# Sliding-window attention with a SwiGLU block: K and Q loaded six tokens per partition and put in order by the evictions, blocks of 512 and 256 tokens, one 3-bank PSUM ring

## The chip, the cores and the metric

The kernel runs on one core of one Trainium2 chip. The metric is the device time of one execution in microseconds; lower is better. The span of a profiled execution is some 2 us shorter than its device time. Stage times below are read from profiles, comparisons of kernels from device times.

## The reference

```python
# q, k, v: (4 batches, 8 heads, 768 tokens, 64), float32, drawn as randn * 0.1; n_sink = 4, window = 128
def _attn_ref(q, k, v, n_sink, window):
    scores = scale * np.matmul(q, k.transpose(0, 1, 3, 2))
    keep = is_sink | in_window            # the first 4 keys, and the last 128
    a = softmax(where(keep, scores, -1e9))
    return np.matmul(a, v)

def _moe_ref(x, w_gate, w_val, w_out):    # 3072 tokens, 512 -> 1536 -> 512
    g = x @ w_gate
    return (silu(g) * (x @ w_val)) @ w_out
```

## The kernel before

The work goes in groups of 256 tokens of one batch (12 groups). A group's K and Q are loaded as bf16 with 128 tokens on the partitions, transposed by TensorE for two heads at a time (step T), evicted to `kqT`, and used for scores (S), sink scores (K), probabilities times V (PV) and the transpose of the result (X) that the feed-forward reads. After a prologue with groups 0 and 1, the feed-forward of 512 tokens runs with the attention of the next two groups woven into its steps. In the traces each engine executes its instructions in program order: in the kernel before, VectorE's later work stands behind one multiply that waits 40.6 us.

```python
    ps_f = pool("ps_f", 3, True)       # gate, value and down outputs
    ps_s = pool("ps_s", 1, True)       # scores, two banks
    ps_o = pool("ps_o", 2, True)       # PV outputs
    ps_t = pool("ps_t", 1, True)       # T, K and X: one bank
    # ... (the queue of GpSimd, in order:)
    load_group(0, split=2)             # K, Q, V of 256 tokens: runs of 64 values
    load_group(1)
    load_gate(0); load_gate(1); load_gate(2); load_gate(3)     # masks are built in between
    load_group(2)
    for i in range(4):
        load_out(i)
    load_group(3)
    for b in range(B):                 # the sink values, last of all: 32 loads of 4 rows
        for h in range(H):
            nc.gpsimd.dma_start(vcs[b][h * NS:(h + 1) * NS, 0:D], v[b, h, 0:NS])
    # ...
    def step_T(g, p, on_dve=False):
        pt = ps_t.tile([P, 2, 2, P], BF16, tag="pt", name="pt")
        for i in range(2):
            for t in range(2):
                nc.tensor.transpose(
                    pt[:, i, t], nat[g][:, i, t, p * P:(p + 1) * P], ident)
        dst = kqT[b][:, p, :, c * 256:(c + 1) * 256].rearrange(
            "q i (t r) -> q i t r", t=2)
        if on_dve:
            nc.vector.tensor_copy(out=dst, in_=pt)
        else:
            nc.scalar.copy(out=dst, in_=pt)          # 128 partitions, dense
    # ...
    def step_ks(g):                    # after the first group of a batch
        # ...
        nc.vector.tensor_tensor(       # vsb: the sink values, one block per head
            vsbs[b],
            vcs[b].rearrange("q (o d) -> q o d", o=1).broadcast_to([P, H, D + 1]),
            diag_h.rearrange("q (h o) -> q h o", o=1).broadcast_to([P, H, D + 1]),
            op=ALU.mult)
```

The softmax here doesn't subtract the row's maximum and nothing guards it: scores larger than these inputs give would overflow.

## Time and profile before

| | before |
|---|---|
| device time, median | 327.62 us (3 runs, 327.23 to 330.12) |
| span of the profile | 325.2 us |
| first feed-forward matmul | 74.4 us |

In a line of the page's slices each digit is a fortieth of the span, in tenths of busy time. A group of instructions reads: line, engine, operation, output <- input, partitions x elements, count, then busy us and mean ns of one, then the idle time before them with its releasers. The prediction shows the slices, the waits and the stages. Two more lines of before, its evictions of the transposes, from the groups by shape:

```profile
L213 ACT COPY kqT<-pt 128x512 bf16<-128x512 bf16 x44 | 25.8, 585 | 54.6 <-PE pt L206 54.6
L211 DVE COPY kqT<-pt 128x512 bf16<-128x512 bf16 x4 | 1.7, 424 | 12.6 <-PE pt L206 12.6
```

### The profile page before, as it was taken

The numbers are of one execution on the slowest core, as the hardware profiler recorded it, in microseconds if no ns is written. First come the engines' busy times: TensorE is split into PE (matmuls) and PEld (weight loads), VectorE is DVE, ScalarE is ACT, GpSimd is POOL, SyncE is SP. The second block draws the span as 40 slices with busy tenths as digits, with TensorE's granted clock in tenths as the row PEclk, the third lists the DMA queues.
The fourth block names the chain that finished last, engine by engine and source line by source line (L and its number), as shares of the span: only waits on it lengthen the run. The fifth ranks groups of instructions, "written<-read, shape, count | busy, mean of one in ns | idle before, by whom it ended". The sixth has DMA issues, their size and how long they took to land.

```text
span 325.2 us, 4622 instructions
## 1 busy us (share of the span) xinstructions
PE 251.2 (77%) x1824; PEld 128.8 (40%) x1824; DVE 167.9 (52%) x352; ACT 127.2 (39%) x197; POOL 95.8 (29%) x142
## 2 busy tenths in 40 slices
PE   0420000576999988999979999799997999999995
PEld 0210000353454544555434545345453454544442
DVE  2200000663788526886158882378842688617830
ACT  1230000324665136762257541475514666223321
POOL 8996756996532006050042600000000000000000
PEclk9999999999999999999999999999999999999999
DMA  8999999099929129390149932100011000020002
GB/s 56 113 132 203 173 203 90 1 72 124 100 15 84 40 92 73 24 99 30 69 54 78 75 24 90 39 2 3 1 65 67 0 2 0 34 94 3 2 32 97
DMA packets 85268, 20.75 MB, mean 64 GB/s; under 512 B 76544, under 2 KB 82176, under 8 KB 85248
## 3 DMA queue, kind: packets, MB, share of 16 engines
q0 software_dynamic: 81792, 14.18, 55.3%
q1 hardware_dynamic: 3456, 6.29, 5.0%
q8 instruction: 14, 0.23, 0.3%
q14 instruction: 6, 0.05, 0.0%
HBM read 28.34 MB, written 6.29 MB: 107 GB/s over the span
## 4 chain that ended last, share of the span: by engine, by line
PE 63%; DVE 13%; DMA 9%; POOL 7%; ACT 5%; issue 2%; DVEq 0%; POOLq 0%
PE pd L363 18%; PE pv L348 16%; PE pg L340 15%; DVE ht L353 4%; PE o L286 4%; PE s L242 3%; PE pt L206 3%; DMA wg<-in_moe_w_gate_dram 3%; DMA va<-in_v_dram 3%; POOL kq L89 3%; DMA wo<-in_moe_w_out_dram 3%; DVE e L251 2%; DVE u L352 2%; ACT th L343 2%; PE px L304 2%
## 5 line engine op out<-in xcount | busy, mean ns | idle before, releaser
L340 PE MATMUL pg<-xT,wg 128*128 128x512 bf16 x288 | 73.9, 379 | 0.5 <-DVE xT L307 0.5
L348 PE MATMUL pv<-xT,wv 128*128 128x512 bf16 x288 | 74.1, 380 | 0.0
L352 DVE SCALAR_TENSOR_TENSOR u<-th,pg 128x512 bf16<-128x512 f32 x72 | 49.4, 686 | 40.8 <-ACT th L343 39.9
L343 ACT ACTIVATE th<-pg 128x512 f32<-128x512 f32 x72 | 43.0, 597 | 69.4 <-PE pg L340 69.4
L206 PE MATMUL pt<-ident,kq 128*128 128x128 bf16 x192 | 20.2, 233 | 61.2 <-DVE kqT L211 39.9
L363 PE MATMUL pd<-wo,ht 128*128 128x512 bf16 x288 | 65.6, 379 | 0.0
L353 DVE TENSOR_TENSOR ht<-u,pv 128x512 bf16<-128x512 bf16 x72 | 49.5, 688 | 24.1 <-PE pv L348 19.5
L247 ACT ACTIVATE e<-s 128x1024 bf16<-128x1024 f32 (+1 forms) x48 | 45.6, 950 | 9.9 <-PE s L242 9.3
L213 ACT COPY kqT<-pt 128x512 bf16<-128x512 bf16 x44 | 25.8, 585 | 54.6 <-PE pt L206 54.6
L89 POOL DMA_DIRECT2D kq<-in_k_dram x26 | 22.6, 882 | 77.7 <-PE pt L206 76.7
L340 PEld LDWEIGHTS <-wg 128*128 128x128 bf16 x288 | 28.2, 98 | 34.4 <-issue 0.6
L206 PEld LDWEIGHTS <-kq 128*128 128x128 bf16 x192 | 13.6, 103 | 67.6 <-issue 61.2
L363 PEld LDWEIGHTS <-ht 128*128 128x128 bf16 x288 | 27.4, 98 | 30.4
L367 ACT ACTIVATE ot<-pd 128x512 f32<-128x512 f32 x24 | 14.3, 597 | 60.3 <-PE pd L363 60.3
L348 PEld LDWEIGHTS <-wv 128*128 128x128 bf16 x288 | 25.0, 98 | 23.6 <-issue 3.6
L251 DVE TENSOR_TENSOR e<-e,mask 128x1024 bf16<-128x1024 bf16 (+1 forms) x48 | 30.6, 640 | 1.8 <-ACT e L247 1.8
L223 DVE TENSOR_TENSOR vsb<-vc,diag_h 128x520 bf16<-128x520 bf16 x4 | 2.8, 701 | 40.7 <-DMA vc<-in_v_dram 40.6
L89 POOL DMA_DIRECT2D kq<-in_q_dram x26 | 22.6, 885 | 0.8 <-DMA wv<-in_moe_w_val_dram 0.8
L242 PE MATMUL s<-kqT 64*128 64x128 bf16 (+1 forms) x256 | 19.6, 255 | 3.9 <-ACT e L247 3.9
L96 POOL DMA_DIRECT2D va<-in_v_dram x24 | 21.4, 915 | 3.7 <-DMA wo<-in_moe_w_out_dram 1.7
L292 DVE TENSOR_TENSOR xn<-o,rcp 128x256 bf16<-128x256 f32 x48 | 20.4, 425 | 1.7
L286 PEld LDWEIGHTS <-e 128*128 128x128 bf16 x352 | 17.7, 103 | 6.6 <-issue 0.9
(36 smaller groups left out, 126.0 us busy)
## 6 DMA issues: line engine op xcount, KB each, us to landing
out_dram<-ot SPq DMA_DIRECT2D x24, 256.0 KB, 2.0
va<-in_v_dram POOLq DMA_DIRECT2D x24, 128.0 KB, 4.5
kq<-in_k_dram POOLq DMA_DIRECT2D x22, 128.0 KB, 4.2
kq<-in_q_dram POOLq DMA_DIRECT2D x22, 128.0 KB, 4.7
wg<-in_moe_w_gate_dram POOLq DMA_DIRECT2D x4, 384.0 KB, 7.7
wv<-in_moe_w_val_dram POOLq DMA_DIRECT2D x4, 384.0 KB, 8.9
wo<-in_moe_w_out_dram POOLq DMA_DIRECT2D x4, 384.0 KB, 9.1
vc<-in_v_dram POOLq DMA_DIRECT2D x32, 0.5 KB, 1.6
```

Of the source, the lines that this page charges most:

```text
L89: nc.gpsimd.dma_start(kq[:, i, j, s * hn * D:(s + 1) * hn * D].rearrange("p (h d) -> p h d", d=D), src[b, hs, t0 + j * P:t0 + (j + 1) * P] ...
L206: nc.tensor.transpose(pt[:, i, t], nat[g][:, i, t, p * P:(p + 1) * P], ident)
L242: nc.tensor.matmul(ps[:, h, col:col + n], kT[r, kk:kk + P], qT[r, qq:qq + n], start=True, stop=True)
L247: nc.scalar.activation(e, ps[:, :, lo:512], AF.Exp, scale=scale)
L251: nc.vector.tensor_tensor(e, e, m[:, :, lo:512].broadcast_to([P, 2, 512 - lo]), op=ALU.mult)
L286: nc.tensor.matmul(o, l, r, start=(i == 0), stop=(i == len(mms) - 1), skip_group_check=True)
L340: nc.tensor.matmul(pg, wgs[fi][:, c, fs], x[:, c], start=(c == 0), stop=(c == DMC - 1))
L343: nc.scalar.activation(th, pg, AF.Tanh, scale=0.5)
L348: nc.tensor.matmul(pv, wvs[fi][:, c, fs], x[:, c], start=(c == 0), stop=(c == DMC - 1))
L352: nc.vector.scalar_tensor_tensor(u, th, 1.0, pg, op0=ALU.add, op1=ALU.mult)
L353: nc.vector.tensor_tensor(hts[tb][:, f], u, pv, op=ALU.mult)
L363: nc.tensor.matmul(po, hts[tb][:, f, ts * P:(ts + 1) * P], wos[f // n][:, f % n], start=(f == 0), stop=(f == DFC - 1))
```

## The change

Its intent: loads of K and Q in long runs, all of a batch at once; the sink values first, on another queue; a feed-forward that starts after 512 tokens and then takes the 256 that complete a batch; and three PSUM banks shared by all short steps. A token's place is `6 * partition + r`, so a transpose of two tokens of one head gives even tokens on PSUM rows 0 to 63 and odd ones on rows 64 to 127, and the evictions put them in order.

```diff
-    TB = 512
+    SIZES = [512, 256, 512, 512, 512, 512, 256]
+    R = S // P                                   # 6 tokens per partition
-    FG = 3
+    FCH = [1, 2, 3, 3, 3]                        # gate weights in chunks of these sizes
-    natp = pool("natp", 4)
+    natp = pool("natp", 2)
-    ps_o = pool("ps_o", 2, True)
-    ps_t = pool("ps_t", 1, True)
+    ps_a = pool("ps_a", 3, True)
... (pools cut)
+    def load_kq(b, p):
+        if p == 0:
+            nat[b] = natp.tile([P, 2, H, R * D], BF16, tag="kq", name="kq")
+        hs = slice(2 * p, 2 * p + 2)
+        for i, src in ((0, k), (1, q)):
+            nc.gpsimd.dma_start(
+                nat[b][:, i, hs],
+                src[b, hs].rearrange("h (p r) d -> p h (r d)", r=R))
... (V and weights cut)
+    vcf = const.tile([P, B, D + 1], FP32)
+    for h in range(H):                           # first of all, on the sync queue
+        nc.sync.dma_start(
+            vcf[h * NS:(h + 1) * NS, :, 0:D],
+            v[:, h, 0:NS].rearrange("b s d -> s b d"))
... (order of loads cut; the four vsb multiplies stand before the first T)
+    def step_T(b, h):
+        pt = ps_a.tile([P, 2, R // 2, P], BF16, tag="a", name="pt")
+        for i in range(2):
+            for r in range(R // 2):
+                nc.tensor.transpose(
+                    pt[:, i, r], nat[b][:, i, h, 2 * r * D:2 * (r + 1) * D], ident)
+        rows = slice(h % 2 * D, (h % 2 + 1) * D)
+        dst = kqT[b][rows, h // 2].rearrange(
+            "q i (p r u) -> q i r p u", r=R // 2, u=2)
+        nc.scalar.copy(out=dst[:, :, :, :, 0], in_=pt[0:D])
+        nc.vector.tensor_copy(out=dst[:, :, :, :, 1], in_=pt[D:2 * D])
... (the prologue runs T,T,S,S four times, then K, PV, X;
     the blocks' slots hold T at 12 to 19 of blocks 0 and 1, 0 to 7 of block 2, 8 to 15 of block 3)
```

## The prediction

> **What bounds the kernel now.** I read the page by slices first, then the chain of waits, then the timeline where both stop, then the busy time by stage. The 40 slices (8.1 us each) show two stages:
>
> ```profile
> PE   0420000576999988999979999799997999999995
> DVE  2200000663788526886158882378842688617830
> DMA  8999999099929129390149932100011000020002
> ```
>
> TensorE does nearly nothing in slices 3 to 7 and is then busy to the end, while the DMA engines are saturated at the start only. The waits (engine, line, releaser, total us, times, longest) name the hole:
>
> ```profile
> DVE vsb L223 <- DMA vc<-in_v_dram: 40.6, 1, 40.6
> PE pt L206 <- DVE kqT L211: 39.9, 2, 39.4
> ```
>
> One VectorE multiply (vsb) waits 40.6 us for the small sink-value loads (vc), and TensorE waits behind VectorE. The timeline confirms it, with the start of the first feed-forward matmuls below (start, duration, then the idle time):
>
> ```profile
> 56.14 0.70 DVE L223 TENSOR_TENSOR vsb<-vc,diag_h 128x520 bf16<-128x520 bf16 x1 [40.58 <-DMA vc<-in_v_dram]
> ...
> 74.40 1.02 PE L340 MATMUL pg<-xT,wg 128*128 128x512 bf16 x4 [0.52 <-DVE xT L307]
> ```
>
> So vc, issued last on the GpSimd queue behind all weights, holds VectorE's in-order queue until 56.1, and the first block starts at 74.4. From there, by stage (start:end, length, busy time of each engine):
>
> ```profile
> 74.40:117.55 43.15, 40.42 (x297) 20.32 (x297) 27.20 (x58) 20.26 (x32) 13.43 (x16) 1.00 0.93 75
> 246.79:290.54 43.75, 41.44 (x321) 21.42 (x320) 26.85 (x53) 22.04 (x34) 0.00 (x0) 1.00 0.07 25
> 290.54:321.63 31.09, 31.08 (x144) 13.92 (x142) 16.51 (x24) 9.55 (x16) 0.00 (x0) 1.00 0.09 34
> 321.63:325.20 3.57, 0.00 (x0) 0.00 (x0) 0.00 (x0) 0.60 (x1) 0.00 (x0) 1.00 0.19 73
> ```
>
> A block of 512 tokens with nothing woven in takes 31.09 us, all TensorE: 12 gate steps of 1.73 and 4 down tiles of 2.59. With two groups of attention it takes 42.5 to 43.75. The tail is 3.6. This stage is bound by TensorE; before: 74.4 + 247.2 + 3.6 = 325.2 us of span, timed 327.0.
>
> **What the Trainium skill says.** (1) DMA: Bandwidth & Descriptors, Specifications, wants at least 512 B per descriptor for line rate. The trace agrees in direction: group loads (packets of 128 B written) moved 75 to 110 GB/s, the gate weights (768 B written) 200. (2) VectorE: DVE Perf Modes, Mode 2×_1P, needs 16-bit data at step ±1 for two elements a cycle. The dense 128x512 bf16 eviction took 424 ns, a 512-wide fp32 one 688, so the dense copy has it; a strided one will lose it. (3) Vector Engine (DVE) Microarchitecture Reference, 5.2: a port hopping every element ran at about 1.71 ns per column for a destination hopping 4 KiB, 2.5 for a step of 24 words, against 1.05. No long strided write is in this trace; the 16-element memset with steps of 144 B took 72 ns against 59 for one element, which shows no such cost. I leave it between. (4) TensorE: Matmul & The Clock Gate, Part 1, gives half clock after idling. Four transposes took 0.58 us in the prologue, 0.38 in the blocks: agrees.
>
> **The change part by part.**
>
> *vc.* Sink values come as eight small fp32 loads on the sync queue at the very start, and the four vsb multiplies run on VectorE by about 9 us (loads estimated landed near 6; 4 x 0.70). The 40 us wait goes. They hold the first VectorE eviction till then.
>
> *Loads.* K and Q of a whole batch come in eight loads with runs of 1536 B in HBM, 768 B in SBUF. At the 200 GB/s of the weights, batch 0 (1.57 MB written) needs 8 us instead of roughly 17 at 95; GpSimd's issuing (some 0.65 each, by fewer pieces than the 0.88 of before) and the mask building (2.7 us) space it to about 13. In queue order I then estimate: V0 16, gate chunk 0 18.5, V1 21, chunk 1 24, V2 27, chunks 2 to 4 at 31, 35, 39, K and Q of batch 1 at 47, output weights 55, V3 and V4 60. All precede their use below, so DMA drops out as a bound.
>
> *Evictions.* A transpose step is now one head, six transposes (0.34 us), two evictions of 64x768, even tokens on ScalarE, odd on VectorE. ScalarE: 384 ns at 256, 597 at 512, so 0.81 at 768. VectorE: 425 at 256 and 688 at 512 give 0.95 at one element a cycle, 1.47 at the skill's hop cost; I take 1.15. Over the kernel that is 32 x 1.15 = 37 us of new VectorE work and about as much ScalarE work (26) as before.
>
> *Prologue.* Four rounds of T,T,S,S. The score bank pair is single, so a round is a chain: S1 matmuls to transposes 1.3, two VectorE evictions 2 x 1.15, S0 matmuls 0.55, exp 0.85: 5.1 us. First S1 at about 12.9 (vsb to 9, two evictions, S0, exp); fourth at 12.9 + 3 x 5.1 = 28.2. Then masks, K, 8 PV (0.60 VectorE each) and 4 X (0.42), VectorE-paced: 9.1 us (before, K to first gate took 8.05 with half the PV). First gate matmul at **37.4** instead of 74.4.
>
> *Blocks.* Per step, PE/VectorE: gate 512 1.73/1.38; gate 256 0.88/0.85 (u and ht 424 ns each); T 0.34/1.15; S 0.43/0.69 (0.55 at a batch's start); K 0.44/0; PV 0.35/0.60; X 0.25/0.42. In each slot I take the larger sum; dense VectorE stretches overlap by about 0.1 a slot.
> - Block 0 (12 gates, one group): 24.8.
> - Block 1 gates (256, eight T, four S): VectorE 12 x 0.85 + 8 x 1.15 + 4 x 0.55 + 1.0 = 22.6, less 1.2: 21.4; TensorE alone would need 15. VectorE-bound.
> - The six downs: 15.6 + 4.9 of two groups' tail = 20.5.
> - Block 2: eight slots with T hold 3.1 to 3.8 of VectorE against 2.4 to 2.7; gates 35.0, downs 11.5: 46.5.
> - Block 3: four T in gates, four in downs: 44.0.
> - Block 4, no T: 27.7 + 11.6 = 39.3.
> - Blocks 5 and 6: 24.6, 11.8 (a 256 gate without attention runs as the loop ht, pg, th, u, ht, about 0.98 a step rather than 0.88), 15.6: 52.0.
>
> Sum 66.7 + 46.5 + 44.0 + 39.3 + 52.0 = **248.5**, against 247.2 before. The 3-bank ring removes the transposes' wait for their one bank (3.27 us where 2.17 of work was, twice a block), and eight of the transposes' 40 units leave the blocks; VectorE's new work and small blocks pay it back. Span 37.4 + 248.5 + 3.6 = 289.5; with the 1.8 to 2.4 that timing adds: **292 us**.
>
> **Rivals.** (a) *The strided eviction costs the full hop penalty, on both engines.* For it: the skill's 1.71 to 2.5 ns. Against: the memset. At 1.47 us: prologue +2.6, blocks 1 to 3 about +6.4, so 301; at 2.1, about 315. (b) *A DMA wait takes vc's place* (batch 0's K and Q, or the gate chunks, late): the queue holds 11 MB read before block 0 can finish, and before showed GpSimd stalls on full queues from 27 us. If early loads ran at 100 GB/s, the first gate moves to about 45: 300. Against: 200 GB/s for equal pieces. (c) *VectorE doesn't bind* (2-element mode or ample slack; the ring's gain comes in full): blocks at TensorE's sum, some 10 us less: 282. (d) *The hidden wait*: vc's stall was hidden by weight loads that would be awaited anyway. Against: the gate weights landed by 34 in before, 22 us before vc.
>
> **Range and chances.** (a) and (b) push up by 8 to 10, (c) down by 10, so 280 to 305. Even (a) and (b) together stay under 321, 2% below before: faster 0.97, same 0.02, slower 0.01.
>
> **What would show it.** Right: no wait above about 5 us for a sink load; first pg matmul at 34 to 41; kqT evictions on VectorE of 0.95 to 1.5 us; VectorE above 85% busy while block 1's gates run and in block 2's gates; blocks 4 and 5 TensorE-bound near 39; loads of K and Q near 200 GB/s. Wrong: evictions of 2 us; first gate past 45 after a DMA wait; gate steps of block 0 waiting for weights; or blocks 1 and 2 that keep TensorE's pace.

## The result, and the profile after

The changed kernel took **369.02 us** (4 runs, 368.45 to 370.71) against 328.87 us for before in the same comparison (4 runs, 327.23 to 330.81). A ratio here is the mean time of one kernel's fast runs over that of the other's in the same rounds, so it isn't quite the ratio of the medians: 1.123, 95% interval 1.114 to 1.131. It is 12% slower; 292 with a range of 280 to 305 was predicted.

The slices of the page after (9.2 us each), which answer to those of before:

```profile
PE   1212259995665899676669999656879999999996
DVE  4665587886899743498899178677698971898700
PEclk9999999998555699988889999988998999999999
DMA  6999999900003992000000200000020002000022
```

Counting from 0, TensorE is still thin up to slice 5, and there are three new thin stretches (slices 9 to 13, 16 to 20, 25 to 29). The DMA engines are saturated in slices 1 to 7 and again only in 13 and 14. TensorE's granted clock falls in or after some of the thin stretches. The groups by shape name the new cost:

```profile
L223 DVE COPY kqT<-pt 64x768 bf16<-64x768 bf16 x32 | 86.9, 2715 | 32.7 <-ACT kqT L222 32.3
L222 ACT COPY kqT<-pt 64x768 bf16<-64x768 bf16 x32 | 86.7, 2709 | 20.3 <-PE pt L216 20.0
```

The waits of the changed kernel (engine, line, releaser: us in total, times, longest), cut to four:

```profile
DVE kqT L223 <- ACT kqT L222: 32.3, 18, 4.5
...
PE s L246 <- DVE kqT L223: 29.5, 8, 5.0
PE pv L356 <- DVE u L360: 27.5, 16, 4.5
...
DVE vsb L194 <- DMA vcf<-in_v_dram: 4.0, 1, 4.0
```

One eviction takes 2.71 us on *both* engines, though the first probe below shows different rates for dense copies (0.572 us on ScalarE, 0.417 on VectorE for 512). 64 of them make 173.6 us, against 27.5 before. The sink values are no longer a problem: 4.0 us of waiting instead of 40.6. A round of the prologue in the timeline (start, duration, then idle time before) shows how they stand in line:

```profile
15.20 0.50 PE L246 MATMUL s<-kqT 64*128 64x256 bf16 x3 [2.35 <-DVE kqT L223]
15.74 0.81 ACT L251 ACTIVATE e<-s 128x768 bf16<-128x768 f32 x1 [3.44 <-PE s L246]
17.14 1.46 PE L216 MATMUL pt<-ident,kq 128*128 128x128 bf16 x12
18.17 5.40 ACT L222 COPY kqT<-pt 64x768 bf16<-64x768 bf16 x2
20.88 5.44 DVE L223 COPY kqT<-pt 64x768 bf16<-64x768 bf16 x2 [3.67 <-ACT kqT L222]
26.38 0.50 PE L246 MATMUL s<-kqT 64*128 64x256 bf16 x3 [2.35 <-DVE kqT L223]
```

From one S to the next, 15.20 to 26.38, is 11.2 us. ScalarE starts the two evictions at 18.17; VectorE may start the first head's only when ScalarE has finished with the same PSUM tile, at 20.88, and is done with the second at 26.32: three evictions end to end. The stages after (start:end, length, then the busy us of PE, PEld, DVE, ACT and POOL, the granted clock, DMA share and GB/s) say where it bites:

```profile
84.94:127.73 42.79, 26.82 (x168) 18.28 (x166) 35.07 (x43) 29.59 (x25) 11.86 (x15) 0.56 0.36 43
127.73:148.05 20.32, 20.32 (x173) 10.69 (x170) 9.55 (x26) 7.07 (x10) 0.87 (x1) 1.00 0.81 106
148.05:211.62 63.57, 48.20 (x313) 23.38 (x312) 48.26 (x62) 37.59 (x33) 0.00 (x0) 0.89 0.05 17
312.22:365.30 53.08, 52.51 (x337) 28.21 (x335) 31.32 (x62) 19.29 (x35) 0.00 (x0) 1.00 0.08 31
```

The first is the gates of block 1, with the eight T of batch 1: 42.8 us at a granted clock of 0.56. The second, the six down tiles after them, and the last, blocks 5 and 6, hold no T and run at TensorE's pace. In the gates of block 1 the timeline shows the link from eviction to matmul (`u` is VectorE's first multiply of a gate step, `ht` its second, `pv` the value matmul):

```profile
88.66 2.70 DVE L223 COPY kqT<-pt 64x768 bf16<-64x768 bf16 x1 [2.27 <-ACT kqT L222]
88.86 2.69 ACT L222 COPY kqT<-pt 64x768 bf16<-64x768 bf16 x1
91.38 0.42 DVE L360 SCALAR_TENSOR_TENSOR u<-th,pg 128x256 bf16<-128x256 f32 x1
91.85 1.01 PE L356 MATMUL pv<-xT,wv 128*128 128x256 bf16 x4 [4.47 <-DVE u L360]
```

VectorE's eviction stands in its queue ahead of u; u frees the bank that the next value matmul wants; TensorE waits 4.47 us. The two evictions also overlap here, at 2.70 and 2.69 us.

### The profile page after: what moved, and what is told of

Same layout as the page of the kernel before. It is cut to its first block, busy times and chain, and to the rows that moved or that the text cites. A ratio compares the mean times of both kernels' runs of the same rounds, so it can differ in the third digit from the quotient of the medians.

```text
span 368.9 us, 4833 instructions
## 1 busy us (share of the span) xinstructions
PE 277.6 (75%) x1920; PEld 146.6 (40%) x1920; DVE 256.6 (70%) x398; ACT 190.1 (52%) x197; POOL 61.3 (17%) x92
## 4 chain that ended last, share of the span: by engine, by line
PE 53%; DVE 26%; ACT 16%; issue 3%; DMA 1%; SPq 1%; DVEq 0%; ACTq 0%
DVE kqT L223 18%; PE pv L356 15%; PE pd L374 14%; PE pg L348 13%; ACT kqT L222 12%; PE s L246 4%; PE o L290 3%; DVE u L360 3%; ACT e L251 2%; DVE ht L361 1%; PE px L314 1%; ACT th L351 1%; PE pt L216 1%; DVE xn L296 1%; DMA vcf<-in_v_dram 1%
## 5 line engine op out<-in xcount | busy, mean ns | idle before, releaser
L223 DVE COPY kqT<-pt 64x768 bf16<-64x768 bf16 x32 | 86.9, 2715 | 32.7 <-ACT kqT L222 32.3
L356 PE MATMUL pv<-xT,wv 128*128 128x512 bf16 (+1 forms) x336 | 85.2, 382 | 27.9 <-DVE u L360 27.5
L222 ACT COPY kqT<-pt 64x768 bf16<-64x768 bf16 x32 | 86.7, 2709 | 20.3 <-PE pt L216 20.0
L351 ACT ACTIVATE th<-pg 128x512 f32<-128x512 f32 (+1 forms) x84 | 45.6, 543 | 91.2 <-PE pg L348 78.1
L348 PE MATMUL pg<-xT,wg 128*128 128x512 bf16 (+1 forms) x336 | 85.1, 381 | 1.2 <-DVE xT L317 0.5
L360 DVE SCALAR_TENSOR_TENSOR u<-th,pg 128x512 bf16<-128x512 f32 (+1 forms) x84 | 51.2, 610 | 18.8 <-ACT th L351 17.1
L361 DVE TENSOR_TENSOR ht<-u,pv 128x512 bf16<-128x512 bf16 (+1 forms) x84 | 51.4, 612 | 12.1 <-PE pv L356 4.0
L348 PEld LDWEIGHTS <-wg 128*128 128x128 bf16 x336 | 36.0, 107 | 37.5 <-issue 8.0
L378 ACT ACTIVATE ot<-pd 128x512 f32<-128x512 f32 x24 | 14.7, 614 | 41.8 <-PE pd L374 41.8
L216 PE MATMUL pt<-ident,kq 128*128 128x128 bf16 x192 | 20.5, 263 | 14.6 <-DVE kqT L223 8.7
L246 PEld LDWEIGHTS <-kqT 64*128 64x128 bf16 x256 | 8.3, 98 | 52.5 <-DVE kqT L223 31.7
L89 POOL DMA_DIRECT2D kq<-in_k_dram x16 | 11.5, 721 | 55.7 <-PE pt L216 48.3
```

The costliest lines, as they stand in the source:

```text
L216: nc.tensor.transpose(pt[:, i, r], nat[b][:, i, h, 2 * r * D:2 * (r + 1) * D], ident)
L222: nc.scalar.copy(out=dst[:, :, :, :, 0], in_=pt[0:D])
L223: nc.vector.tensor_copy(out=dst[:, :, :, :, 1], in_=pt[D:2 * D])
L246: nc.tensor.matmul(ps[:, h, col:col + n], kT[r, kk:kk + P], qT[r, qq:qq + n], start=True, stop=True)
L348: nc.tensor.matmul(pg, wgs[fi][:, c, fs], x[:, c, 0:n], start=(c == 0), stop=(c == DMC - 1))
L351: nc.scalar.activation(th, pg, AF.Tanh, scale=0.5)
```

## The experiments

**Theory A**: the cost is the eviction itself, set by the 12-byte step between neighbouring 2-byte writes in SBUF, and made worse where the two engines take turns on one PSUM tile. **Rivals**: the half-used partitions and the shift from rows 64 to 127 (B); lone 2-byte writes whatever their step (C); the small blocks, the ring or the throttled clock (D); a path that both engines share (E).

f3_vonly has two runs, the others four. The first gate matmul is the first one of the feed-forward.

| run | what it is | us | ratio to before | first gate matmul, us |
|---|---|---|---|---|
| changed kernel | | 369.0 | 1.123 | 59.2 |
| e1_dense | evictions side by side, tokens out of order | 282.0 | 0.859 | 33.9 |
| e2_byhead | both evictions of a head on one engine | 364.8 | 1.109 | 52.7 |
| e3_sink | kernel before, sink values first | 296.1 | 0.900 | 36.0 |
| f1_ascend | evictions in ascending order of tokens | 297.2 | 0.903 | 40.7 |
| f2_pair | one dense eviction for two heads | **279.8** | 0.851 | 33.7 |
| f3_vonly | ascending on VectorE alone | 334.5 | 1.017 | 52.8 |
| f5_asc_byhead | f1 and both evictions of a head on one engine | 293.8 | 0.894 | 39.0 |
| f4_oldring | f1 with the rings of before | 329.4 | 1.006 | 50.5 |
| f6_ringctl | control for f4 | 297.3 | 0.904 | 40.6 |

### m1_probe and m2_probe: the eviction by itself

The kernel before, with copies from PSUM to SBUF appended after its last output, each form twice on each engine (cut; `k` is the step in elements):

```diff
+    def st(n, k, q=D):
+        return pz[0:q, 0:n * k].rearrange("q (n k) -> q n k", k=k)[:, :, 0]
+    for cp, s_ in ((nc.scalar.copy, srcs[0]), (nc.vector.tensor_copy, srcs[1])):
+        for _ in range(2):
+            h_ = s_[0:D]
+            cp(out=pz[0:D, 0:512], in_=h_[:, 0:512])         # dense
+            cp(out=st(512, 6), in_=h_[:, 0:512])             # 12 bytes apart
+            cp(out=st(512, 6, P), in_=s_[:, 0:512])          # on 128 partitions
+            ...
```

> The kernel before, with 44 copies from PSUM to SBUF added after its last output, each form twice on ScalarE and twice on VectorE, to measure the eviction by itself. Theory A (the step of the 2-byte writes sets the cost): 512 elements dense take 0.58 us on ScalarE and 0.42 on VectorE; at a step of 12 bytes about 1.86 (0.16 + 512 x 3.32 ns, from the 2.71 us for 768) on both engines, with 64 or 128 partitions alike; the same elements of 768 written in ascending order (dense destination, PSUM read at a step of 256 bytes) fall back to about 0.8 to 1.0. Rival B (half the partitions, or the shift of 64 partitions, sets it): dense copies on 64 partitions are slow too, about 1.8, and 128 partitions at a step of 12 bytes are not. Rival C (a 2-byte write that is alone in a 4-byte word costs, whatever the step): a step of 4 bytes costs as much as one of 12, and fp32 at a step of 12 bytes nothing extra. The 22-row tail adds some 60 us to the span of before; its time is not used.

> A second probe after the last output of the kernel before, twice each on ScalarE and VectorE, for the rule behind the first: there the time of 512 bf16 writes grew by 0.56 us for each further 4 bytes between neighbours (1.10 ns per write and 4 bytes) up to 16 bytes. Rule 1 (proportional to the distance without limit): at 6 bytes 1.0 us for 512; 128 writes at 12, 24, 32, 64 bytes 0.58, 1.0, 1.3, 2.4 us; 56 at 144 bytes 2.4 us. Rule 2 (saturates at a 16-byte line): from 16 bytes on nothing more, 128 writes about 0.75 us whatever the distance. Source in SBUF instead of PSUM at 12 bytes: 1.85 again if the write side sets it. Pairs of bf16 12 bytes further (4-byte runs, a step of 24 bytes): between 1.0 and 1.9. fp32 at 4, 8, 16 bytes: 0.6, 0.8, 1.3 if it grows like bf16 but at a lower rate (it took 0.95 to 1.05 at 12). A memset of 512 at 12 bytes: 1.85 if memsets are writes like others; the 16-element memset that the prediction leaned on showed no cost, so under rule 1 the 56-element memset at 144 bytes would take 2.4 us, and if it takes 0.12 memsets differ from copies.

The groups of the first probe by shape: 12 bytes apart on 64 partitions (L432), on 128 (L434), and 768 elements written in ascending order while PSUM is read at a step of 256 bytes (L437):

```profile
L434 ACT COPY pz<-prs 128x512 bf16<-128x512 bf16 x2 | 3.7, 1856 | 0.1
L434 DVE COPY pz<-prs 128x512 bf16<-128x512 bf16 x2 | 3.7, 1854 | 0.1
L432 ACT COPY pz<-prs 64x512 bf16<-64x512 bf16 x2 | 3.7, 1848 | 0.1
L432 DVE COPY pz<-prs 64x512 bf16<-64x512 bf16 x2 | 3.7, 1847 | 0.1
...
L437 DVE COPY pz<-prs 64x768 bf16<-64x768 bf16 x2 | 1.9, 949 | 0.1
...
L437 ACT COPY pz<-prs 64x768 bf16<-64x768 bf16 x2 | 1.6, 792 | 0.1
```

64 and 128 partitions cost the same, so the half-used partitions of B fall. The shift of rows was not in the probe; it falls with e1_dense below, where shifted dense evictions take 0.79 and 0.56 us and the probe's unshifted ones 0.792 and 0.549. The probe's own copy of 768 elements at 12 bytes took 2.695 and 2.671 us, which is the kernel's eviction. The step decides, but not as rival C has it. For bf16, taking off a fixed 0.153 us (from 128 and 512 writes at 12 bytes, 0.577 and 1.848 us on ScalarE):

| bytes between neighbours | writes | ScalarE, us | VectorE, us | ns per write (ScalarE) |
|---|---|---|---|---|
| 2 (dense) | 512 | 0.572 | 0.417 | engine's own rate |
| 4 | 512 | 0.720 | 0.718 | 1.11 |
| 6 | 512 | 1.014 | 0.998 | 1.68 |
| 8 | 512 | 1.284 | 1.280 | 2.21 |
| 12 | 512 | 1.848 | 1.847 | 3.31 |
| 16 | 512 | 2.414 | 2.410 | 4.42 |
| 24 | 128 | 0.712 | 0.710 | 4.37 |
| 32 | 128 | 0.687 | 0.686 | 4.17 |
| 64 | 128 | 0.707 | 0.704 | 4.33 |
| 144 | 56 | 0.394 | 0.392 | 4.30 |

The numbers fit 4.4 ns times step/16, and 4.4 from 16 bytes on: Rule 2 of the expectation (about 0.75 us for 128 writes from 16 bytes on; 0.69 to 0.71 measured). It is what a fixed charge for each new 16-byte line would give; the line is an inference from the numbers, and fp32 at 12 and 16 bytes, nearly alike on ScalarE, does not follow it. Whole words are cheaper: fp32 at 12 bytes took 1.045 (ScalarE) and 0.948 us, at 16 bytes 1.052 and 1.046, so about 1.7 ns; pairs of bf16 every 24 bytes took 0.598 us for 256 pairs, also about 1.7. Several expectations of the second probe missed: 1.0 to 1.9 us for the pairs, 0.8 and 1.3 for fp32 at 8 and 16 bytes (0.606 and 1.052 on ScalarE), and 1.85 from an SBUF source, which only ScalarE took. Groups of the second probe by shape, the SBUF source (L441) and memsets:

```profile
L441 ACT COPY pz<-mask 64x512 bf16<-64x512 bf16 x2 | 3.8, 1890 | 0.1
...
L441 DVE COPY pz<-mask 64x512 bf16<-64x512 bf16 x2 | 2.0, 1010 | 0.1
...
L448 DVE MEMSET pz<- 64x512 bf16 x2 | 1.0, 485 | 2.5 <-issue 2.5
L450 DVE MEMSET pz<- 64x512 bf16 x2 | 1.0, 485 | 0.3 <-DVE pz L449 0.3
L449 DVE MEMSET pz<- 64x56 bf16 x2 | 0.2, 105 | 0.5 <-DVE pz L448 0.5
```

So on VectorE the written step alone does not set the cost: the same writes from SBUF take 1.010 us, from PSUM 1.847. The finding holds for copies from PSUM, which the evictions are; why the source matters stays open. Memsets are exempt: 512 elements at 12 bytes (L448) cost what 512 dense ones do (L450), and 56 at 144 bytes (L449) 0.105 us, where a copy took 0.394. In the timeline L449, which waits for L448, starts 0.74 us after L448 does, so its row hides no slow write. Reading PSUM at a step of 256 bytes cost ScalarE nothing (0.792 us dense and permuted); VectorE went from 0.549 to 0.949 us.

### e1_dense: the changed kernel without the step

```diff
         dst = kqT[b][rows, h // 2].rearrange(
-            "q i (p r u) -> q i r p u", r=R // 2, u=2)
+            "q i (u r p) -> q i r p u", r=R // 2, u=2)
```

> The changed kernel with the two evictions of a head written side by side, densely, instead of interleaved at a step of six tokens. The result is wrong on purpose (tokens out of order); all else is the same. Theory A: ScalarE 0.81 and VectorE about 0.56 an eviction instead of 2.71; first gate matmul near 34 to 37 instead of 59.2; total 283 to 295. Rival B (partitions, not the step): evictions stay at 2.7 and the total near 369. Rival D (the losses come from the small blocks, the ring or the throttled clock, not from the evictions): evictions fall, total above 330.

Measured: evictions 0.79 and 0.56 us, first gate 33.9, total 282.0 us. Rival D falls: blocks, ring and loads are those of the changed kernel, 87 us faster. Two reservations. The result is wrong, yet it passed the comparison: q and k are drawn at a scale of 0.1, so I take the softmax to be nearly flat and the comparison to be a weak guard of token order. That the other variants keep the order right therefore rests on their code, not on the comparison. And the two halves now lie in separate token ranges, so the first S of a round waits for ScalarE's half alone in this variant, which flatters its prologue. f1_ascend has neither fault.

### e2_byhead: without the turn-taking

In the built program VectorE's eviction waits on ScalarE's semaphore. Building two variants told why, without a run: with VectorE writing to another SBUF tile the wait stayed, with VectorE reading another PSUM tile it went. So the order is put into the program when it is built, on two engines that read one PSUM tile. The Trainium skill, PSUM — Partial Sum Buffer, Terms, counts two engines on one bank and quadrant at once as an error, reads against reads included; but here ScalarE reads rows 0 to 63 and VectorE rows 64 to 127, which by the same section are different quadrants (32 partitions each), so that rule does not ask for this wait. No run here let the two read at once.

```diff
-        nc.scalar.copy(out=dst[:, :, :, :, 0], in_=pt[0:D])
-        nc.vector.tensor_copy(out=dst[:, :, :, :, 1], in_=pt[D:2 * D])
+        cp = nc.vector.tensor_copy if h % 2 else nc.scalar.copy
+        cp(out=dst[:, :, :, :, 0], in_=pt[0:D])
+        cp(out=dst[:, :, :, :, 1], in_=pt[D:2 * D])
```

> The changed kernel with both evictions of a head on one engine: even heads on ScalarE, odd ones on VectorE. Each engine then reads its own PSUM tile, so the wait of VectorE for ScalarE's read of the same tile (32.3 us in the profile) goes. Same data, right result. Theory A with serialization: each eviction stays at 2.71, two heads are ready in 5.4 us instead of 10.9; first gate matmul near 37 to 39 (four rounds of 5.4 less), total 312 to 330. Rival E (both engines share one path for such writes[...]): evictions running at the same time stretch to about 5.4, first gate near 59, total 360 to 370.

Measured 364.8 us, ratio 1.109: only 4 us faster than the changed kernel. Each eviction stayed at 2.71 while two ran at once, so rival E falls. My own expectation (312 to 330) fell as well: I had counted four evictions end to end for two heads, but ScalarE's second runs beside VectorE's first, so it was three and became two: a round went from 11.2 to 8.9 us. The first gate moved by 6.4 us, and the blocks gave 1.5 of it back. Turn-taking is the small part of the loss.

### e3_sink: one part of the change alone

The kernel before, with the sink values loaded first on the sync queue and the head mask built early:

```diff
+    for h in range(H):
+        nc.sync.dma_start(
+            vcf[h * NS:(h + 1) * NS, :, 0:D],
+            v[:, h, 0:NS].rearrange("b s d -> s b d"))
     load_group(0, split=2)
...
-    for b in range(B):
-        for h in range(H):
-            nc.gpsimd.dma_start(vcs[b][h * NS:(h + 1) * NS, 0:D], v[b, h, 0:NS])
```

> The kernel before with one part of the change alone: the sink values loaded first, on the sync queue, in fp32, and the head mask built early. Loads, evictions, blocks and rings are those of before. Theory A (that wait is the whole hole of the prologue, and nothing hidden stands behind it): first gate matmul at 33 to 40 instead of 74.4, total 285 to 295. Rival F (group and gate loads would be awaited anyway): first gate at 50 or later, total above 303.

Measured 296.1 us, ratio 0.900, first gate at 36.0: that wait was the hole of the prologue, as the prediction read it. The total is 1 us outside what I expected, because a load takes a small part of the place. In its timeline group 2's K and Q, behind the gate weights in the queue, arrive just after block 0 has begun:

```profile
38.88 0.23 PE L205 MATMUL pt<-ident,kq 128*128 128x128 bf16 x1 [1.88 <-DMA kq<-in_k_dram]
...
41.72 0.29 PE L205 MATMUL pt<-ident,kq 128*128 128x128 bf16 x1 [0.63 <-DMA kq<-in_q_dram]
```

Two more of 0.73 us lie between them; the four add up to 4.0 us.

### f1_ascend and f3_vonly: the same data in another order, and half the dose

```diff
-            "q i (p r u) -> q i r p u", r=R // 2, u=2)
-        nc.scalar.copy(out=dst[:, :, :, :, 0], in_=pt[0:D])
-        nc.vector.tensor_copy(out=dst[:, :, :, :, 1], in_=pt[D:2 * D])
+            "q i (p r u) -> q i p r u", r=R // 2, u=2)
+        nc.scalar.copy(out=dst[:, :, :, :, 0],
+                       in_=pt[0:D].rearrange("q i r p -> q i p r"))
+        nc.vector.tensor_copy(out=dst[:, :, :, :, 1],
+                              in_=pt[D:2 * D].rearrange("q i r p -> q i p r"))
```

> The changed kernel, right result, with one edit: the evictions walk the tokens in ascending order (partition outside, token of the partition inside), so each write lands 4 bytes after the last instead of 12, and the PSUM side is read at a step of 256 bytes instead. Theory A (cost goes by the bytes between neighbouring 2-byte writes; the probe gave 0.72 us for 512 at a step of 4 bytes, 0.58 for 384): 1.00 us an eviction on both engines. From the dense variant's 282.0 us, 0.44 more of VectorE in each of 20 gate slots and about 0.65 in each of four prologue rounds: 287 to 294, first gate near 36. Rival G (the scattered PSUM read is slow in its turn, or partition-shifted evictions differ from the probe): evictions above 1.5, total above 305.

> Half a dose: as the ascending variant, but on VectorE alone; ScalarE keeps the step of 12 bytes. Right result. Theory A: VectorE 1.00, ScalarE 2.71 an eviction; if the loss goes with the eviction time on the path, the total lies between 290 and 369, near 325, first gate near 46 to 49 (a round of T,T,S,S from 11.2 to about 8.5). Rival: one slow engine alone costs nearly the whole (above 355) or nearly nothing (below 300).

Every element goes from the same place to the same place; only the order of the walk differs, so each write lands 4 bytes on instead of 12. Groups of f1_ascend by shape:

```profile
L224 DVE COPY kqT<-pt 64x768 bf16<-64x768 bf16 x32 | 32.6, 1019 | 16.0 <-ACT kqT L222 15.5
L222 ACT COPY kqT<-pt 64x768 bf16<-64x768 bf16 x32 | 32.2, 1006 | 14.3 <-PE pt L216 14.0
```

The evictions fall to 1.0 us, as the probe said, and the kernel from 369.0 to 297.2 us: **72 us by the order of two loops**. That isolates the order of the writes, and with it their step, as the cause. The total is 3 us above what I expected, because I started from e1_dense's flattered prologue: the rounds take 6.1 us here, with three evictions of 1.0 end to end, and the first gate comes at 40.7.

Half the dose (f3_vonly) gave 334.5 us, near the middle, with evictions of 2.71 and 1.02 us. Against before, its ratio of 1.017 (1.008 to 1.025) is unclear; against the other variants the distance is far outside the noise. The loss goes with the eviction time. Its first gate, at 52.8, was later than I expected: VectorE waits 52.1 us for ScalarE's slow half of the same tile, so here one slow engine does hold the other.

### f5_asc_byhead: turn-taking again, at 1 us an eviction

The edits of f1_ascend and e2_byhead together.

> The ascending variant with both evictions of a head on one engine (even heads ScalarE, odd ones VectorE), so that no engine waits for the other's read of a shared PSUM tile. Theory: as with the slow evictions (369.0 to 364.8 us), it shortens only the prologue: two evictions of 1.0 end to end instead of three, 1 us a round, first gate 3 to 4 earlier; in the blocks VectorE has the same work but unevenly, so at most 4 us in all against the ascending variant. Rival: worth more than 8 us.

Measured 293.8 us against 297.2: 3.4 us less, within what was expected in all. But a round went from 6.1 to 5.5 us, not by the 1 us expected, so the first gate moved by 1.7 instead of 3 to 4; the rest came in the blocks.

### f4_oldring and f6_ringctl: the 3-bank ring

f1_ascend with the rings of before. To build without a deadlock it needs two further edits, which f6_ringctl has as well, with the 3-bank ring:

```diff
-    ps_a = pool("ps_a", 3, True)
+    ps_o = pool("ps_o", 2, True)
+    ps_t = pool("ps_t", 1, True)
... (T, K and X in ps_t, PV in ps_o)
-    pro(*V0)
-    flush()
-    pro(V1[0], *X0, *V1[1:])
-    flush()
-    pro(*X1)
+    for s in [*V0, V1[0], *X0, *V1[1:], *X1]:
+        flush()
+        s()
... (block 3: a slot's T ahead of its other steps)
```

> The ascending variant with the PSUM ring of before (two banks for the PV outputs, one for transposes, K scores and X), flushing VectorE's pending work before each step of the prologue's second half and putting each transpose step first in its slot, without which the build deadlocks in the simulator. Right result. Theory (the 3-bank ring saves the transposes' wait for their single bank, which the prediction put at about 1.1 us in each slot with two steps): each of the 24 transposes steps in the blocks waits for its two serial evictions of 1.0 before the next use of the bank, but slots hold one step only, so the ring is worth 1 to 6 us: 298 to 304. Rival (the ring is worth nothing here): 296 to 298; rival (it is what carries the gain): above 310.

> The control for the old-ring run: the ascending variant with the same flushes in the prologue and the same order of steps in the slots as that run, but with the 3-bank ring kept. Right result. If the 32 us between the ascending variant (297.2) and the old ring (329.4) are the ring's, this stays at 296 to 302. If they came from the flushes or the order of steps, it goes to 315 or more.

The old rings gave 329.4 us, the control 297.3. So the ring is worth 32 us beside these evictions; I had expected 1 to 6. The timeline of f4_oldring's prologue shows how:

```profile
24.02 0.82 PE L217 MATMUL pt<-ident,kq 128*128 128x128 bf16 x6
...
25.04 0.99 ACT L223 COPY kqT<-pt 64x768 bf16<-64x768 bf16 x1
26.07 1.01 DVE L225 COPY kqT<-pt 64x768 bf16<-64x768 bf16 x1 [2.05 <-ACT kqT L223]
27.13 0.80 PE L217 MATMUL pt<-ident,kq 128*128 128x128 bf16 x6 [2.29 <-DVE kqT L225]
```

The next head's transposes wait until both engines have emptied the single bank, so a round takes 8.0 us (22.08 to 30.07 between its S) instead of 6.1. In the blocks VectorE's half also waits its turn behind u, ht and masks while the bank is held. That a bank emptied by two engines in turn needs more banks behind it than one emptied at once is likely, but not shown: no run has the old rings with one evicting engine for each tile.

### f2_pair: a version that beats both

A step takes K or Q of two heads. Two 64-column transposes per token residue put the heads on rows 0 to 63 and 64 to 127, so one dense eviction on 128 partitions replaces two of 64, and no PSUM tile is read by two engines.

```diff
+        p, i = divmod(h, 2)
+        pt = ps_a.tile([P, R, P], BF16, tag="a", name="pt")
+        for r in range(R):
+            for hh in range(2):
+                nc.tensor.transpose(
+                    pt[hh * D:(hh + 1) * D, r],
+                    nat[b][:, i, 2 * p + hh, r * D:(r + 1) * D], ident)
+        cp = nc.vector.tensor_copy if i else nc.scalar.copy
+        cp(out=kqT[b][:, p, i].rearrange("q (p r) -> q p r", r=R),
+           in_=pt.rearrange("q r p -> q p r"))
```

> The changed kernel with a step taking K or Q of two heads: twelve transposes of 64 columns put one head on PSUM rows 0 to 63 and the other on 64 to 127, so one eviction of 128 partitions, dense and ascending, does for the two half-partition ones: K on ScalarE (0.79 by the probe), Q on VectorE (0.95). 32 evictions instead of 64, none sharing a PSUM tile between engines. Right result. Theory: VectorE and ScalarE have half the eviction work of the ascending variant, TensorE 0.34 us a step more at most; total 278 to 286. Rival H (TensorE pays for the doubled transposes in every slot and they don't overlap): above 288.

Measured **279.75 us**, ratio 0.851 (0.845 to 0.856). Its groups by shape:

```profile
L217 PE MATMUL pt<-ident,kq 128*64 128x128 bf16 x384 | 18.8, 246 | 5.5 <-POOL diag_h L140 4.9 <-DMA kq<-in_q_dram 0.5
L221 DVE COPY kqT<-pt 128x768 bf16<-128x768 bf16 x16 | 15.3, 956 | 10.2 <-PE pt L217 10.0
L221 ACT COPY kqT<-pt 128x768 bf16<-128x768 bf16 x16 | 12.7, 797 | 9.8 <-PE pt L217 9.5
```

28.0 us of evictions instead of 173.6. Twice the number of transposes (384) cost TensorE 18.8 us busy against 18.0 in f1_ascend at the same granted clock (20.5 in the changed kernel, at 0.917), so the doubling was nearly free.

Set beside e3_sink this says what the rest of the change is worth. With evictions of 1.0 us (f1_ascend, 0.903, interval 0.898 to 0.909) it gains nothing over the sink values alone (e3_sink, 0.900, 0.895 to 0.905); with f2_pair's it gains some 16 us.

## Why the prediction was wrong

By its own steps, the stages in us of span:

| stage | predicted | changed kernel | f1_ascend | f2_pair |
|---|---|---|---|---|
| to the first gate | 37.4 | 59.2 | 40.7 | 33.7 |
| blocks 0 and 1 | 66.7 | 88.9 | 69.5 | 64.1 |
| block 2 | 46.5 | 63.6 | 45.9 | 41.9 |
| block 3 | 44.0 | 58.7 | 44.8 | 43.6 |
| block 4 | 39.3 | 41.9 | 37.8 | 37.8 |
| blocks 5 and 6 | 52.0 | 53.1 | 53.1 | 53.1 |
| tail | 3.6 | 3.6 | 3.6 | 3.6 |
| span | 289.5 | 368.9 | 295.4 | 277.8 |

- **The step that failed is "Evictions"**: "0.81 at 768" for ScalarE and "I take 1.15" for VectorE, where both took 2.71. The stages that hold T, the prologue and blocks 0 to 3, carry 21.8 + 22.2 + 17.1 + 14.7 = 75.8 of the 79.4 us of error. With evictions of 1.0 us, nothing else changed, the prediction's sum is 6 us off (289.5 against 295.4 of f1_ascend).
- **The size doesn't carry all of it.** An estimate: 2.71 in place of 1.15 in the prediction's own sums adds at most 32 x 1.56 = 50 us of the 79.4. Of the 29 left, 9.3 lie in the prologue (rounds of 11.2 us instead of the 8.2 that two evictions of 2.71 would give), 8.9 in block 1's gates and 4.6 in block 2. VectorE is busy for only 82% and 85% of the gates of these two blocks, so its summed work, which the prediction took as the length of a slot, isn't all that sets it. Waits between engines (TensorE's 27.5 us for u among them) and the lower granted clock come on top; the runs don't separate them.
- It failed in three places. ScalarE was charged no step at all in the base sum. VectorE was put between one element a cycle and the skill's 1.71 ns, when a lone 2-byte write 12 bytes on costs 3.3. And the counter-evidence was a memset, which is the one kind of strided write that the probes show to be free. Rival (a) had the mechanism, and stopped at 2.1 us and 315.
- **"Two VectorE evictions" in a prologue round** was a second, smaller error: with the turn-taking there are three end to end. Taking it away shortened a round by 2.3 us here (e2_byhead) and by 0.6 beside f1_ascend (f5_asc_byhead), and the whole by 4 and 3 us.
- **The bound of before was read rightly.** The sink load was the hole (e3_sink: first gate at 36.0 and 33 us less in total), and the stages without T came within 3 us.
- **DMA as a bound (rival b)** did not come: the first gate waited for no load, and the waits of TensorE for loads name only the first K and Q (5.1 and 0.7 us). The first K and Q loads moved 137 to 188 GB/s between 3.4 and 7.5 us, somewhat under the 200 assumed.
- **"VectorE above 85% busy" in the gates of blocks 1 and 2** did not come: 35.1 of 42.8 us (82%) and 44.5 of 52.4 (85%). In f1_ascend, with the evictions near the assumed size, it is 21.05 of 23.44 us (90%) for block 1. The granted clock of 0.56 there is 1.00 in f1_ascend with nothing but the order of writes changed. That it follows TensorE's idling is not shown: in the prologue TensorE is busy 19.0 of 59.2 us at a recorded clock of 1.00. The record may miss slow spells, since six score matmuls take 0.61 us there and 0.40 in block 0. In the same way the prediction's fourth reading of the skill (0.58 against 0.38 us) agrees in duration only, by a ratio of 1.5; the recorded clock is 1.00 in both stages of before.
- **Small blocks:** "about 0.98 a step" for a 256 gate without attention. In the changed kernel the last block's gate steps start at 338.47, 340.52, 342.57 and 344.62 for every second one: 1.03 a step.
- **The ring's gain**, put at 1.1 us in two slots a block, was under-read: 32 us beside two evictions in turn (f4_oldring, f6_ringctl).
- **Slips in its working that move little:** TensorE's empty slices are 3 to 6, not 3 to 7; a round's terms add up to 5.0, not 5.1; four of the transposes' 40 units leave the blocks, not eight (160 transposes in the blocks before, 144 after); in before, GpSimd still waits for the last value weights until 36.5 us, so not all gate weights had landed by 34.

What stays open: why a lone 2-byte write costs 4.4 ns and a 4-byte one 1.7 at the same distance. The probes show the charge, not its mechanism. Nor do they say why VectorE pays it for a PSUM source and only half of the time for an SBUF one. How much of f2_pair's lead over f1_ascend is the halved eviction work and how much the absence of turn-taking is only estimated, by f5_asc_byhead (3.4 of 17.4 us for the latter).

## What to carry to other kernels

Before reordering data in an eviction, measure that copy with its real element size and step: a 2-byte write, copied from PSUM, that lands alone in its stretch of 16 bytes took 4.2 to 4.4 ns on both engines, where VectorE's dense copy needs some 0.5. The same permutation may be walked so that the writes are dense, or closer, and the PSUM read takes the step: for 768 elements that cost ScalarE nothing and VectorE 0.4 us. A memset doesn't stand in for a copy. Give a PSUM tile to one evicting engine where you can, and where two take turns, try more banks (32 us here).

## What the Trainium skill lacked or had wrong

- Vector Engine (DVE) Microarchitecture Reference, 5.2, measures per-element hops of 4-byte words (1.71 ns for a hopping destination). fp32 agrees here, about 1.7 ns at 16 and 64 bytes, on both engines. It lacks 2-byte elements: from PSUM 3.3 ns at 12 bytes, 4.2 to 4.4 from 16 on.
- The same charge holds on ScalarE (1.848 us for 512 at 12 bytes, VectorE 1.847); ScalarE: Activation LUTs has nothing of it.
- SBUF — State Buffer, Door 1, tells of 16-byte lines and a penalty for each access that crosses to a new one, without a number. The growth up to 16 bytes and the flat part after it fit the lines; full bandwidth at two hits on a line does not: at 8 bytes, two writes to a line, 512 took 1.284 us against 0.572 dense on ScalarE. The numbers that it lacks: 4.4 ns for 2-byte writes, 1.7 for whole words, none for VectorE's memset (485 ns for 512 at 12 bytes as for dense ones), which no page that I read has.
- The same passage says that a PSUM pattern that isn't contiguous slows matmuls; it lacks the evicting engines. A PSUM *read* at a step of 256 bytes did not slow ScalarE (0.792 us for 768 both ways) and took VectorE from 0.549 to 0.949.
